# A chunked attention feeding a two-layer network: value products by chunk on 64 partitions, in a TensorE step of their own

## The chip, the cores and the metric

The kernel runs on one core of a Trainium2 chip. A core has TensorE (PE; its weight loads are shown apart, as PEld), VectorE (DVE), ScalarE (ACT), GpSimd (POOL) and SyncE (SP, which issues the DMA transfers here). The metric is the time of one execution in device microseconds. All times are in microseconds (us) unless marked ns.

## The reference, cut to what matters

```python
# attention: batch 4, heads 8, sequence 768, head width 64, 8 memory keys
chunk, left_ctx, right_ctx = (32, 16, 8)
for c in range(768 // chunk):
    k_full = concat(mem_k, k[c_start - 16 : c_end + 8])      # 8 + 56 = 64 keys, fewer at the ends
    v_full = concat(mem_v, v[c_start - 16 : c_end + 8])
    scores = scale * q_c @ k_full.T
    a = exp(scores - max(scores))
    a = a / (sum(a) + 1e-09)
    out[c_start:c_end] = a @ v_full
x = out as 3072 tokens x 512
# two-layer network
h = x @ w_in                                  # 512 -> 2048
g = maximum(h, 0) + alpha * minimum(h, 0)
return g @ w_out                              # 2048 -> 512
```

Each chunk of 32 queries sees 64 keys (8 of the memory, 16 on the left, its own 32, 8 on the right). All is float32.

## The kernel before, in words

**Blocks, slices, units.** The 3072 tokens are 8 blocks of 384. The hidden width of 2048 is 16 slices of 128, so the network is 128 pairs (block, slice). One pair is: `up`, 12 matmuls that move 384 columns (L614, into `h_ps`); `below` and `bend` (ACT L623, DVE L626), which form `g`; a split of `g` into a high part `gh` (L632) and a low part `gl` (L636); and `down`, 9 matmuls that move 512 columns (L644, into the banks `o_ps`). Below, "a slice" is also the time that TensorE takes for one such pair. The attention of a block is 4 units, one for each pair of heads, 32 units in all. A unit's outputs are also split in two (`xh` on ACT L408, `xl` on DVE L412), and `up` of the block reads both. The weights arrive packed and are decoded once, slice by slice, by `decode` (DVE and ACT, L556 to L583), while block 0 is computed.

**Units 0 to 7** (blocks 0 and 1) are done by `windows` at the start, by products of all of TensorE's 128 rows: scores L271, transposes L480, values L493. Their queries, keys and values come as `early` (L424).

**Units 8 to 31** go through four steps. `head_products` makes the scores of 12 chunks and two heads (L289, 24 matmuls on 64 partitions, into two PSUM banks `s0` and `s1`). `scores` takes the maxima (DVE L299 to L313) and the exponentials (ACT L320). `weights` divides (DVE L334, L337, then POOL L340) and copies a part into a padded tile `e2` (ACT L344). `turn` transposes the weights on DVE into a zeroed tile `pt` (L361, 14 pieces from the list `PIECES`). Each tile of 96 queries then has a window of 128 keys, in which a chunk's 64 weights stand beside zeros. `value_products` (L375) makes 8 matmuls of 128 rows, 64 output columns and 96 moving columns into one bank `a`. `zero` clears `e2` and `pt` once on POOL.

**What sets the order.** Nothing is ordered by hand inside a slice. `Plan` takes steps with an engine, an assumed cost, what they read and write, and a due time, and sends them in the order of a list schedule; each engine then runs its own list strictly in that order. `ORDER` lists the pairs (block, slice). Block 1's first `NJOINT` = 9 slices run interleaved with block 0's, `LAG` = 2 slices behind; their `down` adds up in the banks `s0`, `s1` and `a`, and ACT copies the sums out before block 2's units need these banks. `begins(u)` is the place at which a unit's scores are due; from block 3 on the four units of the next block begin at places -1, 3, 7 and 11. Weights and turn follow `DUE_WEIGHTS` = 3 slices after that and the values `DUE_VALUES` = 4 slices after, which is where the next unit begins. `attend` puts both into one TensorE step:

```python
def products():
    for u in olds:
        value_products(u)
    for u in news:
        head_products(u)
```

Of the kernel before, what the change touches and what calls it, by code (L numbers as in the profile page):

```python
# [9 lines left out]
F32 = mybir.dt.float32  # L10
# [55 lines left out]

NJOINT, LAG = 9, 2
ORDER = []
# [15 lines left out]

DUE_WEIGHTS, DUE_VALUES = 3, 4

# [70 lines left out]
def body(ctx: ExitStack, tc: tile.TileContext, qvw, kw, first, w_in, w_out, alpha, out):  # L157
# [26 lines left out]
    eye = const.tile([P, P], F32, name="eye")  # L184
    pts, zeroed = [], {}

# [33 lines left out]
    def sets(u):  # L220

        return u % NKB
# [21 lines left out]
    def load_v(u):  # L244
        blk, pr = divmod(u, NPAIR)

        def load():
            state[u]["v"] = ld.tile([P, NT, 2, D], F32, name="v_t")
            nc.sync.dma_start(out=state[u]["v"],
                              in_=qvw[blk, pr, :, BT:].rearrange("p (t h d) -> p t h d", t=NT, h=2))  # L250

        step(SP, 0.75, load, writes=["v"])

# [23 lines left out]

    def head_products(u):

        st = state[u]  # L280
        st["s"] = [ps_s.tile([P, 512], F32, name="s_ps", tag=f"s{h2}")[:, :NJ * KW].rearrange("p (n k) -> p n k", n=NJ)
                   for h2 in range(2)]
        for n in range(NJ):
            for g in range(4):
                t, j = SLOT[(g, n)]
                c = t * NJ + j
                for h2 in range(2):
                    rows = slice(h2 * D, (h2 + 1) * D)
                    nc.tensor.matmul(  # L289
                        out=st["s"][h2][g * CH:(g + 1) * CH, n],  # L290
                        lhsT=qs[sets(u)][rows, c * CH:(c + 1) * CH],
                        rhs=kbs[sets(u)][rows, t, STARTS[j]:STARTS[j] + KW],
                        start=True, stop=True,
                    )
# [35 lines left out]
    def weights(u):  # L330
        st = state[u]

        def guard():
            nc.vector.tensor_scalar(out=st["den"], in0=st["den"], scalar1=1e-9, scalar2=None, op0=ALU.add)  # L334

        def inverse():
            nc.vector.reciprocal(out=st["den"], in_=st["den"])  # L337

        def scale():
            nc.gpsimd.tensor_tensor(out=st["e"], in0=st["e"], in1=st["den"].broadcast_to([P, NJ * 2, KW]),  # L340
                                    op=ALU.mult)

        def spread():
            nc.scalar.copy(out=zeroed["e2"][:, :, NM:NM + CH], in_=st["e"][:, :, :CH])  # L344
# [4 lines left out]
        step(ACT, 0.37, spread, reads=e_keys(u), writes=["e2"], rest=due(u, DUE_WEIGHTS))  # L349

    TURNS = [(g, j, n0, n1, t0) + piece
             for g in range(4)
             for j, n0, n1, t0 in ([(g, 0, NJ, 0)] if g < NJ else [(n, n, n + 1, NT - 1) for n in range(NJ)])
             for piece in PIECES[j]]
    TURNS.sort(key=lambda x: x[5])

    def turn(u):
        st = state[u]

        def go(g, j, n0, n1, t0, src, half, quad):  # L360
            nc.vector.transpose(  # L361
                out=pts[u % NPT][quad * CH:(quad + 1) * CH, j, t0:t0 + n1 - n0].rearrange("p t h q -> p (t h) q"),
                in_=(st["e"], zeroed["e2"])[src][g * CH:(g + 1) * CH, 2 * n0:2 * n1, half * CH:(half + 1) * CH],
            )

        for i, x in enumerate(TURNS):
            step(DVE, 0.37 if x[3] - x[2] > 1 else 0.235, partial(go, *x), reads=["e2"] if x[5] else e_keys(u),
                 writes=[("pt", u % NPT, i)], rest=due(u, DUE_WEIGHTS))

    def value_products(u):  # L370
        st = state[u]
        st["a"] = ps_a.tile([P, 512], F32, name="a_ps", tag="a")
        for t in range(NT):
            for h2 in range(2):
                nc.tensor.matmul(  # L375
                    out=st["a"][h2 * D:(h2 + 1) * D, t * TQ:(t + 1) * TQ],
                    lhsT=st["v"][:, t, h2, :],
                    rhs=pts[u % NPT][:, :, t, h2, :],
                    start=True, stop=True,
                )  # L380

    def attend(place, olds, news):

        def products():
            for u in olds:
                value_products(u)
            for u in news:
                head_products(u)

        reads, writes = [], []  # L390
        for u in olds:
            reads += ["v"] + [("pt", u % NPT, i) for i in range(len(TURNS))]
            writes.append("a")
        for u in news:
            reads += [("q", sets(u)), ("k", sets(u))]
            writes += [("s", 0), ("s", 1)]
# [3 lines left out]
    def split(u, ak="a"):  # L400

        st = state[u]

        slot = u % NX

        def high():
            st["xh"] = xp.tile([P, BT], F32R, name="xh", tag=f"xh{slot}")
            nc.scalar.copy(out=st["xh"], in_=st["a"][:, :BT])  # L408

        def low():  # L410
            xl = xp.tile([P, BT], F32R, name="xl", tag=f"xl{slot}")
            nc.vector.tensor_tensor(out=xl, in0=st["a"][:, :BT], in1=st["xh"].bitcast(F32), op=ALU.subtract)  # L412
            xs[u] = (st["xh"], xl)

        xh, xl = ("xh", slot), ("xl", slot)
        step(ACT, 0.48, high, reads=[ak], writes=[xh])
        step(DVE, 0.56, low, reads=[ak, xh], writes=[xl])

# [11 lines left out]
    def windows(u):  # L430
# [56 lines left out]
        def values():  # L487
            pool, tag = (ps_o, "o2") if u % 2 else (ps_a, "a")
            st["a"] = pool.tile([P, 512], F32, name="a_ps", tag=tag)
            v = early[u % NSET][:, NQ + NT * NKT:].rearrange("p (t h d) -> p t h d", t=NT, h=2)  # L490
            for t in range(NT):
                for h2 in range(2):
                    nc.tensor.matmul(  # L493
                        out=st["a"][h2 * D:(h2 + 1) * D, t * TQ:(t + 1) * TQ],
                        lhsT=v[:, t, h2, :],
                        rhs=st["et"][:, t // 2, :, t % 2, h2, :],
                        start=True, stop=True,
                    )
# [12 lines left out]
        step(PE, 0.85, values, reads=[("q", u % NKB), ("fv", u % NSET)], writes=[ak], rest=due(u, 1))  # L511
        split(u, ak)
# [88 lines left out]
    def hidden(blk, f, first_f, last_f):  # L601
# [51 lines left out]
        def add_up():  # L653
            for ks in [[k] for k in range(NK)] if f < 2 else [list(range(NK))]:
                step(PE, 0.521 * len(ks), partial(up, ks),
                     reads=[("w", 0, f, 0), ("w", 0, f, 1)] + [(x, x_slot + k) for k in ks for x in ("xh", "xl")],
                     writes=[hk], rest=rest(place))
# [66 lines left out]
    for u in range(NWIN):  # L724
        unit_begins(u)
    step(POOL, 3.0, zero, writes=["e2"] + [("pt", i, j) for i in range(NPT) for j in range(len(TURNS))] + [("ew", i) for i in range(NPT)])
    for f in range(NF - NSET, NF):
# [48 lines left out]
def _layout(q, k, v, mem_k, mem_v, moe_w_in, moe_w_out, moe_alpha):  # L776
# [17 lines left out]
    for h in range(2):  # L794
# [3 lines left out]
    kfirst = kfirst.reshape(NBLK, NPAIR, P, NT * NKT)[:nwin]  # L798
    vparts = vwin.reshape(NBLK, NPAIR, P, NV)
    return dict(  # L800
        qvw=np.concatenate([qT.reshape(NBLK, NPAIR, P, BT), vparts], axis=3),
        kw=np.ascontiguousarray(kwin).reshape(NBLK, NPAIR, P, NT, NKT),
# [21 lines left out]
```

## Time and profile before

| | before |
|---|---|
| median of 3 runs | 614.57 (614.47 to 614.58) |
| the profiled execution's own time | 614.44 |
| its span in the profile | 612.7 |
| TensorE matmuls busy | 604.1 (99%) |
| TensorE weight loads busy | 532.5 (87%) |
| VectorE busy | 405.0 (66%) |
| ScalarE busy | 215.4 (35%) |
| GpSimd busy | 34.3 (6%) |

The span is the time between the first and the last instruction that the profiler saw. The profiled execution lies 0.13 under the median and 1.7 over its own span. A matmul in the profile has a start and a modelled end; consecutive ones overlap, so what a group costs TensorE is read from its first start to the next group's first start. A float32 matmul shows as two passes, each with its own weight load: 8 value matmuls are 16 records, 24 score matmuls are 48. In a row of the timeline the columns are start, length, engine, line, operation, output and inputs, array tile (rows*columns), shape of the moving operand, count, and in brackets an idle time and what ended it.

### The profile page before, as it was taken

To read this page: it belongs to the slowest core of one execution; us is meant where nothing else is said; L and a number is where in the kernel's file an instruction comes from. 1 tells how busy PE (TensorE), PEld (TensorE's weight loads), DVE (VectorE), ACT (ScalarE), POOL (GpSimd) and SP (SyncE) were. 2 spreads that over 40 slices of the span, in tenths; PEclk is the share of its full clock that TensorE was granted. 3 is DMA by queue.
4 is the path that set the end of the run, shared out by engine and by line. 5 is a ranking of instruction groups with operands and counts; after the bars stand their busy time and mean duration, and the time that the engine had idled before them with its cause. 6 is when DMAs were issued, how large, how long until landed. Compare 5 with 4: busy or idle time off the path is not lost.

```text
span 612.7 us, 11586 instructions
## 1 busy us (share of the span) xinstructions
PE 604.1 (99%) x4619; PEld 532.5 (87%) x4622; DVE 405.0 (66%) x1012; ACT 215.4 (35%) x596; POOL 34.3 (6%) x61
## 2 busy tenths in 40 slices
PE   8999999999999999999999999999999999999997
PEld 4779999888888888989888889888889888989996
DVE  5899899767877656766566766556766656633332
ACT  3798787544322222222223122332123222121111
POOL 3320000000000000000000000000000000000000
PEclk9999999999999999999999999999999999999999
DMA  8999300013121111201112001221012100010001
GB/s 351 355 404 407 152 0 1 24 41 123 46 101 49 50 49 50 77 25 50 49 50 101 26 25 49 83 67 50 19 31 101 50 18 18 1 53 1 0 1 51
DMA packets 20934, 48.99 MB, mean 80 GB/s; under 512 B 2448, under 2 KB 5520, under 8 KB 20880
## 3 DMA queue, kind: packets, MB, share of 16 engines
q1 hardware_dynamic: 20880, 48.25, 22.1%
q8 instruction: 36, 0.59, 0.4%
q14 instruction: 18, 0.15, 0.1%
HBM read 41.95 MB, written 6.29 MB: 79 GB/s over the span
## 4 chain that ended last, share of the span: by engine, by line
PE 95%; DMA 2%; DVE 1%; ACT 1%; SPq 0%; issue 0%; DVEq 0%; ACTq 0%
PE h_ps L614 44%; PE o_ps L644 44%; PE a_ps L375 3%; PE s_ps L289 3%; DMA early<-first 2%; PE s_ps L271 0%; PE a_ps L493 0%; PE o_ps L480 0%; DVE w_t L564 0%; ACT qk L485 0%; DVE a L572 0%; SPq L424 0%; ACT a L556 0%; ACT xh L408 0%; PE o_ps L257 0%; DVE w_t L568 0%
## 5 line engine op out<-in xcount | busy, mean ns | idle before, releaser
L614 PE MATMUL h_ps<-xh,w 128*128 128x384 f32 x1024 | 261.7, 336 | 0.0
L644 PE MATMUL o_ps<-w,gh 128*128 128x512 f32 x768 | 240.8, 395 | 0.0
L614 PEld LDWEIGHTS h_ps<-xh,w 128*128 128x128 f32 x1024 | 185.7, 188 | 4.1
L614 PE MATMUL h_ps<-xl,w 128*128 128x384 f32 x512 | 175.0, 342 | 1.2 <-DVE xl L412 1.2
L644 PEld LDWEIGHTS o_ps<-w,gh 128*128 128x128 f32 x768 | 144.1, 188 | 27.7
L623 ACT ACTIVATE g<-h_ps 128x384 f32<-128x384 f32 x128 | 63.4, 495 | 251.8 <-PE h_ps L614 245.6
L644 PE MATMUL o_ps<-w,gl 128*128 128x512 f32 x384 | 149.9, 390 | 0.0
L626 DVE SCALAR_TENSOR_TENSOR g<-g,rise,h_ps 128x384 f32<-128x384 f32 x128 | 78.4, 613 | 97.5 <-ACT g L623 96.7
L361 DVE STREAM_TRANSPOSE pt<-e 32x192 f32<-32x192 f32 (+1 forms) x336 | 99.6, 301 | 11.9 <-POOL e L340 6.6
L614 PEld LDWEIGHTS h_ps<-xl,w 128*128 128x128 f32 x512 | 96.2, 188 | 7.8 <-DVE xl L412 1.3
L644 PEld LDWEIGHTS o_ps<-w,gl 128*128 128x128 f32 x384 | 72.2, 188 | 12.2
L636 DVE TENSOR_TENSOR gl<-g,gh 128x384 fp32r<-128x384 f32 x128 | 71.2, 557 | 5.8 <-ACT gh L632 2.4
L632 DVE CAST gh<-g 128x384 fp32r<-128x384 f32 x104 | 37.3, 360 | 54.4 <-PE o_ps L644 52.7
L320 ACT ACTIVATE e<-s_ps,mx 128x64 f32<-128x64 f32 x144 | 43.3, 321 | 39.6 <-DVE mx L313 39.6
L340 POOL TENSOR_TENSOR e<-e,den 128x384 f32<-128x384 f32 x24 | 19.9, 830 | 467.1 <-DVE den L337 467.1
L408 ACT CAST xh<-a_ps 128x384 fp32r<-128x384 f32 x32 | 15.5, 483 | 53.1 <-PE a_ps L375 49.5
L320 ACT ACTIVATION_READ_ACCUMULATOR e<-s_ps,mx 128x1 f32 x144 | 30.7, 213 | 0.0
L375 PEld LDWEIGHTS a_ps<-pt,v_t 128*64 128x64 f32 x384 | 16.6, 136 | 8.5 <-issue 8.5
L375 PE MATMUL a_ps<-pt,v_t 128*64 128x96 f32 x384 | 21.1, 253 | 0.0
L583 DVE TENSOR_TENSOR w<-a,w 128x1024 fp32r<-128x1024 f32 (+1 forms) x18 | 19.7, 1098 | 1.2 <-ACT w L580 1.1
L572 DVE SCALAR_TENSOR_TENSOR a<-a,w_t 128x1024 int32<-128x1024 int32 (+1 forms) x18 | 20.1, 1116 | 0.2
L564 ACT COPY w_t<-w_t 128x512 int16<-128x512 int16 x14 | 19.4, 1387 | 0.1
(52 smaller groups left out, 277.1 us busy)
## 6 DMA issues: line engine op xcount, KB each, us to landing
w_t<-w_in SPq DMA_DIRECT2D x16, 512.0 KB, 10.2
w_t<-w_out SPq DMA_DIRECT2D x16, 512.0 KB, 10.2
qk<-kw SPq DMA_DIRECT2D x24, 272.0 KB, 3.7
v_t<-qvw SPq DMA_DIRECT2D x24, 256.0 KB, 2.7
out<-o_t SPq DMA_DIRECT2D x24, 256.0 KB, 2.1
early<-first SPq DMA_DIRECT2D x8, 656.0 KB, 6.9
qk<-qvw SPq DMA_DIRECT2D x24, 192.0 KB, 3.7
early<-first SPq DMA_DIRECT2D x8, 256.0 KB, 7.2
```

What stands on the lines that cost most here:

```text
L320: nc.scalar.activation(out=st["e"][:, i], in_=st["s"][h2][:, n], func=AF.Exp, scale=SCALE, bias=st["mx"][:, n, h2:h2 + 1], accum_out=st["d ...
L340: nc.gpsimd.tensor_tensor(out=st["e"], in0=st["e"], in1=st["den"].broadcast_to([P, NJ * 2, KW]), op=ALU.mult)
L361: nc.vector.transpose(out=pts[u % NPT][quad * CH:(quad + 1) * CH, j, t0:t0 + n1 - n0].rearrange("p t h q -> p (t h) q"), in_=(st["e"], zer ...
L375: nc.tensor.matmul(out=st["a"][h2 * D:(h2 + 1) * D, t * TQ:(t + 1) * TQ], lhsT=st["v"][:, t, h2, :], rhs=pts[u % NPT][:, :, t, h2, :], sta ...
L572: nc.vector.scalar_tensor_tensor(out=d["a"], in0=d["a"], scalar=3, in1=d["t"][:, :, :, 1], op0=ALU.logical_shift_left, op1=ALU.bitwise_or)
L583: nc.vector.tensor_tensor(out=d["w"][:, :, 1], in0=d["a"].bitcast(F32), in1=d["w"][:, :, 0].bitcast(F32), op=ALU.subtract)
L614: nc.tensor.matmul(out=h["ps"][:, :BT], lhsT=ws[f, 0][:, wk, k * P:(k + 1) * P], rhs=xs[first + k][xk], start=(k == 0 and n == 0), stop=(k ...
L623: nc.scalar.activation(out=h["g"], in_=h["ps"][:, :BT], func=AF.Relu, scale=-1.0)
L626: nc.vector.scalar_tensor_tensor(out=h["g"], in0=h["g"], scalar=rise[:, f:f + 1], in1=h["ps"][:, :BT], op0=ALU.mult, op1=ALU.add)
L632: copy(out=h["gh"], in_=h["g"])
L636: nc.vector.tensor_tensor(out=h["gl"], in0=h["g"], in1=h["gh"].bitcast(F32), op=ALU.subtract)
L644: nc.tensor.matmul(out=o_ps[tt], lhsT=h[gk][:, tt * P:(tt + 1) * P], rhs=ws[f, 1][:, wk], start=(f == first_f and i == 0), stop=(f == last ...
```

## The change

- **Values by chunk.** `value_products` multiplies each chunk's 64 weights with its own 64 values: 24 matmuls of 64 rows, 64 output columns and 32 moving columns. Chunks of the first half of the block use the array's upper 64 rows and bank `a`; chunks of the second half use the lower 64 rows and the upper columns of the bank that otherwise holds `s1`.
- **Less to prepare.** No padded tile: `e2`, its copy on ACT (`spread`) and the clearing on POOL (`zero`) go. `turn` has 8 transposes of 32x192 in place of 14 pieces. The values come from memory by chunk, so a unit's load `v_t` is 384 KB instead of 256 KB.
- **Split in two.** The outputs lie in two banks, so `xh` and `xl` of units 8 to 31 take two instructions of 192 columns each, on ACT and on DVE.
- **When.** `DUE_WEIGHTS` goes from 3 to 2 and `DUE_VALUES` from 4 to 3: the values are a step of their own, one slice ahead of the next unit's scores. Since both use the bank of `s1`, the scores wait for the split of its half.
- **Start.** `LAG` goes from 2 to 1: block 1's slice f follows block 0's slice f directly.
- **Assumed costs** of the planner for `attend` and `split` change with it.

```diff
-SLOT = {(g, n): ((n, g) if g < NJ else (NT - 1, n)) for g in range(4) for n in range(NJ)}
-PIECES = [[(0, 0, 0), (0, 1, 1)], [(0, 0, 1), (0, 1, 2)], [(1, 0, 2), (1, 1, 1), (0, 1, 3)]]
-NJOINT, LAG = 9, 2
+NJOINT, LAG = 9, 1
-DUE_WEIGHTS, DUE_VALUES = 3, 4
+DUE_WEIGHTS, DUE_VALUES = 2, 3
...
-            state[u]["v"] = ld.tile([P, NT, 2, D], F32, name="v_t")
+            state[u]["v"] = ld.tile([P, 2, NJ, 2, D], F32, name="v_t")
...
-    def head_products(u):
+    def head_products(u, second):
         st = state[u]
-        st["s"] = [ps_s.tile([P, 512], F32, name="s_ps", tag=f"s{h2}")[:, :NJ * KW].rearrange("p (n k) -> p n k", n=NJ)
-                   for h2 in range(2)]
+        st["s"] = [t[:, :NJ * KW].rearrange("p (n k) -> p n k", n=NJ)
+                   for t in (ps_s.tile([P, 512], F32, name="s_ps", tag="s0"), second)]
...
-        def spread():
-            nc.scalar.copy(out=zeroed["e2"][:, :, NM:NM + CH], in_=st["e"][:, :, :CH])
...
-        for i, x in enumerate(TURNS):
-            step(DVE, 0.37 if x[3] - x[2] > 1 else 0.235, partial(go, *x), reads=["e2"] if x[5] else e_keys(u),
+        def go(g, half):
+            quad = g // 2 * 2 + half
+            nc.vector.transpose(
+                out=st["pt"][quad * CH:(quad + 1) * CH, g % 2],
+                in_=st["e"][g * CH:(g + 1) * CH, :, half * CH:(half + 1) * CH],
+            )
+        for i in range(8):
+            step(DVE, 0.37, partial(go, i // 2, i % 2), reads=e_keys(u),
...
-        for t in range(NT):
-            for h2 in range(2):
-                nc.tensor.matmul(
-                    out=st["a"][h2 * D:(h2 + 1) * D, t * TQ:(t + 1) * TQ],
-                    lhsT=st["v"][:, t, h2, :],
-                    rhs=pts[u % NPT][:, :, t, h2, :],
-                    start=True, stop=True,
-                )
+        st["a"] = [(ps_a.tile([P, 512], F32, name="a_ps", tag="a")[:, :BT // 2], slice(0, BT // 2)),
+                   (second[:, BT // 2:BT], slice(BT // 2, BT))]
+        for b in range(2):
+            for n in range(NJ):
+                for h2 in range(2):
+                    for i in range(2):
+                        rows, c = slice(i * D, (i + 1) * D), b * NJ + n
+                        nc.tensor.matmul(
+                            out=st["a"][i][0][h2 * D:(h2 + 1) * D, c * CH:(c + 1) * CH],
+                            lhsT=st["v"][rows, b, n, h2, :],
+                            rhs=st["pt"][rows, b, n * 2 + h2],
+                            start=True, stop=True,
+                        )
...
-        step(PE, 0.85 * len(olds) + 0.67 * len(news) - (0.2 if olds and news else 0.0), products, reads=reads, writes=writes,
+        step(PE, 0.75 * len(olds) + 0.75 * len(news), products, reads=reads, writes=writes,
...
-        step(ACT, 0.48, high, reads=[ak], writes=[xh])
-        step(DVE, 0.56, low, reads=[ak, xh], writes=[xl])
+        for i, ak in enumerate(aks):
+            step(ACT, 0.48 if len(aks) == 1 else 0.34, partial(high, i), reads=[ak], writes=xh + xl if i == 0 else [xh[i]])
+        for i, ak in enumerate(aks):
+            step(DVE, 0.56 if len(aks) == 1 else 0.33, partial(low, i), reads=[ak, xh[i]], writes=[xl[i]])
...
-    def zero():
-        zeroed["e2"] = turned.tile([P, NJ * 2, KW], F32, name="e2", tag="e2")
-        nc.gpsimd.memset(zeroed["e2"], 0.0)
-        for i in range(NPT):
-            pts.append(turned.tile([P, NJ, NT, 2, CH], F32, name=f"pt{i}", tag=f"pt{i}"))
-            nc.gpsimd.memset(pts[i], 0.0)
...
-                 writes=[("s", 0), ("s", 1), "a"] if joint else [("o", tt) for tt in range(NTT)],
+                 writes=[("s", 0), ("s", 1), "a", "a1"] if joint else [("o", tt) for tt in range(NTT)],
```

The order of instructions that comes of it is shown at three places, before and after. In these rows a line of the changed kernel has another number: `up` is L601 there, `down` L631, the scores L280, the values L363, the splits L400 (`xh`) and L404 (`xl`), and the weight decode L551 to L570. A number behind a tile's name tells one use of the tile from the next.

**TensorE, at a unit's values and the next unit's scores.** Before:

```order
L644 MATMUL o_ps_2967<-w_1055,gl_3309 128x512
L644 MATMUL o_ps_2967<-w_1055,gh_3306 128x512 x2
L375 MATMUL a_ps_3362<-pt0_649,v_t_3228 64x96 x8
L289 MATMUL s_ps_3371<-qk1_155 32x64
L289 MATMUL s_ps_3372<-qk1_155 32x64
```

After (the last two of 24 value matmuls, one `up`, the first two of 24 score matmuls):

```order
L363 MATMUL a_ps_3277<-pt_3224,v_t_3115 64x32
L363 MATMUL s_ps_3276<-pt_3224,v_t_3115 64x32
L601 MATMUL h_ps_3306<-xl_2302,w_1059 128x384
L601 MATMUL h_ps_3306<-xh_2301,w_1059 128x384 x2
L601 MATMUL h_ps_3306<-xl_2476,w_1059 128x384
L601 MATMUL h_ps_3306<-xh_2475,w_1059 128x384 x2
L601 MATMUL h_ps_3306<-xl_2696,w_1059 128x384
L601 MATMUL h_ps_3306<-xh_2695,w_1059 128x384 x2
L601 MATMUL h_ps_3306<-xl_2902,w_1059 128x384
L601 MATMUL h_ps_3306<-xh_2901,w_1059 128x384 x2
L280 MATMUL s_ps_3328<-qk0_154 32x64
L280 MATMUL s_ps_3327<-qk0_154 32x64
```

Before, 22 of the 24 units have their values directly ahead of another unit's scores. After, none has; one `up` of 12 matmuls lies between them (in block 2's units, where they are packed closer, an `up`, a `down` or both).

**VectorE, at the end of the windows.** The tiles `xl` here are those of units 4 to 7, `w_t`, `a` and `w` those of the weight decode. Before:

```order
L412 TENSOR_TENSOR xl_619<-a_ps_550,xh_589 128x384
L412 TENSOR_TENSOR xl_627<-a_ps_591,xh_612 128x384
L564 COPY w_t_488<-w_t_488 128x512
L583 TENSOR_TENSOR w_638<-a_525,w_638 128x512
L568 TENSOR_SCALAR w_t_488<-w_t_488 128x1024
L572 SCALAR_TENSOR_TENSOR a_617<-a_617,w_t_488 128x1024
L626 SCALAR_TENSOR_TENSOR g_670<-g_670,rise_151,h_ps_606 128x384
L636 TENSOR_TENSOR gl_696<-g_560,gh_679 128x384
L412 TENSOR_TENSOR xl_700<-a_ps_654,xh_690 128x384
L412 TENSOR_TENSOR xl_703<-a_ps_681,xh_698 128x384
```

After:

```order
L404 TENSOR_TENSOR xl_622<-a_ps_589,xh_621 128x384
L570 TENSOR_TENSOR w_625<-a_558,w_625 128x512
L404 TENSOR_TENSOR xl_645<-a_ps_627,xh_644 128x384
L570 TENSOR_TENSOR w_658<-a_532,w_658 128x512
L404 TENSOR_TENSOR xl_666<-a_ps_647,xh_665 128x384
L623 TENSOR_TENSOR gl_681<-g_607,gh_673 128x384
L551 COPY w_t_507<-w_t_507 128x512
L613 SCALAR_TENSOR_TENSOR g_700<-g_700,rise_151,h_ps_602 128x384
L555 TENSOR_SCALAR w_t_507<-w_t_507 128x1024
L623 TENSOR_TENSOR gl_719<-g_700,gh_706 128x384
L559 SCALAR_TENSOR_TENSOR a_679<-a_679,w_t_507 128x1024
```

The decode of a further slice's weights (`w_t_488` before, `w_t_507` after) and one `g` and `gl` moved from ahead of the last `xl` to behind it.

**SyncE, the first transfers** (1312 elements a partition are a unit's queries and keys, 512 its values). Before:

```order
L424 DMA early_157<-first 128x1312 [waits DMAHW0_49,PE_49]
L533 DMA w_t_243<-w_in 128x1024
L424 DMA early_158<-first 128x1312 [waits DMAHW1_49,PE_49]
L424 DMA early_157<-first 128x512
L424 DMA early_159<-first 128x1312 [waits DMAHW2_49,PE_49]
L424 DMA early_158<-first 128x512
```

After:

```order
L418 DMA early_157<-first 128x1312 [waits DMAHW0_49,PE_49]
L418 DMA early_158<-first 128x1312 [waits DMAHW1_49,PE_49]
L418 DMA early_157<-first 128x512
L418 DMA early_159<-first 128x1312 [waits DMAHW2_49,PE_49]
L418 DMA early_158<-first 128x512
L520 DMA w_t_319<-w_in 128x1024
```

The first 512 KB of weights moved behind four more loads of the windows.

More of the change, by code (lines that the diff above doesn't have):

```diff
@@ L348, in weights @@
         step(POOL, 0.86, scale, reads=den_keys(u), writes=e_keys(u), rest=due(u, DUE_WEIGHTS))
[L349 to L355, printed above, removed]
     def turn(u):
         st = state[u]
-        def go(g, j, n0, n1, t0, src, half, quad):
+        def go(g, half):
+            if (g, half) == (0, 0):
+                st["pt"] = turned.tile([P, 2, NJ * 2, CH], F32, name="pt", tag=f"pt{u % NPT}")
+            quad = g // 2 * 2 + half
@@ L370, in value_products @@
-    def value_products(u):
+                out=st["pt"][quad * CH:(quad + 1) * CH, g % 2],
+                in_=st["e"][g * CH:(g + 1) * CH, :, half * CH:(half + 1) * CH],
+            )
+        for i in range(8):
+            step(DVE, 0.37, partial(go, i // 2, i % 2), reads=e_keys(u),
+                 writes=[("pt", u % NPT, j) for j in range(8)] + [("ew", u % NPT)] if i == 0 else [("pt", u % NPT, i)], rest=due(u, DUE_WEIGHTS))
+    def value_products(u, second):
         st = state[u]
-        st["a"] = ps_a.tile([P, 512], F32, name="a_ps", tag="a")
-        for t in range(NT):
-            for h2 in range(2):
-                nc.tensor.matmul(
-                    out=st["a"][h2 * D:(h2 + 1) * D, t * TQ:(t + 1) * TQ],
-                    lhsT=st["v"][:, t, h2, :],
-                    rhs=pts[u % NPT][:, :, t, h2, :],
-                    start=True, stop=True,
-                )
+        st["a"] = [(ps_a.tile([P, 512], F32, name="a_ps", tag="a")[:, :BT // 2], slice(0, BT // 2)),
[11 more added lines that the diff above has]
+                        )
@@ L382, in attend @@
     def attend(place, olds, news):
         def products():
+            second = ps_s.tile([P, 512], F32, name="s_ps", tag="s1")
             for u in olds:
-                value_products(u)
+                value_products(u, second)
             for u in news:
-                head_products(u)
-        reads, writes = [], []
+                head_products(u, second)
+        reads, writes = [], ["a1", ("s", 1)]
         for u in olds:
-            reads += ["v"] + [("pt", u % NPT, i) for i in range(len(TURNS))]
+            reads += ["v"] + [("pt", u % NPT, i) for i in range(8)]
@@ L488, in values @@
             pool, tag = (ps_o, "o2") if u % 2 else (ps_a, "a")
-            st["a"] = pool.tile([P, 512], F32, name="a_ps", tag=tag)
+            a = pool.tile([P, 512], F32, name="a_ps", tag=tag)
+            st["a"] = [(a[:, :BT], slice(0, BT))]
             v = early[u % NSET][:, NQ + NT * NKT:].rearrange("p (t h d) -> p t h d", t=NT, h=2)
```

46 lines of the change are left out of this document (22 added, 24 removed).

## The prediction

> **What bounds the kernel now.** I read the page's busy times and its chain of waits first, then the sums by stretch of time, then TensorE's timeline around one unit's step, the single lines' durations, and the timelines of all engines in the first 40 us.
>
> ```profile
> span 612.7 us, 11586 instructions
> PE 604.1 (99%) x4619; PEld 532.5 (87%) x4622; DVE 405.0 (66%) x1012; ACT 215.4 (35%) x596; POOL 34.3 (6%) x61
> PE 95%; DMA 2%; DVE 1%; ACT 1%; SPq 0%; issue 0%; DVEq 0%; ACTq 0%
> ...
> 14.10:38.80 24.70, 22.23 (x279) 17.57 (x278) 21.89 (x47) 19.65 (x39) 9.64 (x21) 1.00 0.97 372
> ...
> 38.80:612.70 573.90, 570.19 (x4194) 507.99 (x4194) 375.91 (x945) 190.63 (x549) 19.91 (x24) 1.00 0.18 61
> ```
>
> The two stretches show length, then PE, PEld, DVE, ACT and POOL busy, the granted clock, the DMA share and GB/s. From 38.8 on TensorE is idle for 573.90 - 570.19 = 3.7 us, which is the last store; the clock is 1.00. So whatever this change does there counts only as TensorE time: work taken from DVE, ACT or POOL is worth nothing, and TensorE time is worth all of itself. Before 38.8 it is different: TensorE idles for 24.70 - 22.23 = 2.5 us after 14.1, and DVE (21.89) is as full as TensorE.
>
> **The change part by part. The values' own time.** One step of values and scores, an `up` and a `down` from the chain of waits, and one step of scores alone:
>
> ```profile
> 274.78 0.63 PE L644 MATMUL o_ps<-w,gh 128*128 128x512 f32 x2
> 275.34 0.88 PE L375 MATMUL a_ps<-pt,v_t 128*64 128x96 f32 x16
> 276.15 0.73 PE L289 MATMUL s_ps<-qk 64*32 64x64 f32 x48
> 276.81 0.44 PE L614 MATMUL h_ps<-xl,w 128*128 128x384 f32 x1
> 277.09 0.51 PE L614 MATMUL h_ps<-xh,w 128*128 128x384 f32 x2
> ...
> 58.90 2.10 PE h_ps L614 x12
> 61.00 2.08 PE o_ps L644 x9
> ...
> 119.04 0.51 PE L614 MATMUL h_ps<-xh,w 128*128 128x384 f32 x2
> 119.48 0.72 PE L289 MATMUL s_ps<-qk 64*32 64x64 f32 x48
> 120.14 0.50 PE L644 MATMUL o_ps<-w,gl 128*128 128x512 f32 x1
> 120.47 0.62 PE L644 MATMUL o_ps<-w,gh 128*128 128x512 f32 x2
> ```
>
> Start to start, the values take 276.15 - 275.34 = 0.81 and the scores 276.81 - 276.15 = 0.66. A visit to small array tiles costs more than its body. In the last group the scores start 0.09 later than the next `up` matmul would (119.04 + 2 x 0.175 = 119.39; an `up` matmul follows the last after 2.10 / 12 = 0.175, a `down` matmul after 2.08 / 9 = 0.23), and the second matmul behind them comes 0.33 after the first instead of 0.23. That is 0.09 in and 0.10 out: 0.19 a visit. Values and scores together cost 0.81 + 0.66 + 0.19 = 1.66, the scores alone 0.85.
>
> After the change 22 units that shared a visit make two: 22 x 0.19 = 4.2 us more, if the bodies stay. Two units (of the 24) had their values alone already.
>
> The values' new body no row shows. Each of four array tiles gets 6 matmuls of two passes, so 12 rounds, each a weight load of 64 columns and 32 moving columns. Before there were 8 rounds on two tiles: 0.05 for the first load, 8 x 0.083, and 0.10 to leave. Nearest rows for a round:
>
> ```profile
> L271 PEld LDWEIGHTS s_ps<-early x192: 132/138/169, 5.0 to 22.6; 128*64 128x64 f32 x192
> ...
> L289 PEld LDWEIGHTS s_ps<-qk x1152: 102/106/108, 119.5 to 515.6; 64*32 64x32 f32 x192
> ...
> 21.94 0.34 PE L271 MATMUL s_ps<-early 128*64 128x64 f32 x4
> ...
> 21.94 0.51 PE L271 MATMUL s_ps<-early 128*64 128x64 f32 x10
> ```
>
> The windows' scores (L271, two tiles) load 64 columns and move 64. The group's end goes from 0.34 with 4 passes to 0.51 with 10, so three rounds take 0.17: 0.057 to 0.058 a round. That is a little over the 0.055 of moving 64 columns (0.083 x 64 / 96). It is also what the load lasts: a load of 64 columns takes 138 ns against 106 ns for 32, so 32 columns more are 32 ns, and 64 columns hold the tile for 55 to 64 ns. Halving the moving columns therefore shortens a round only until the load ends it. With 0.058: 0.05 + 11 x 0.058 + 0.03 + 0.02 (four tiles start one after another) + 0.10 = 0.84.
>
> The other end is the scores' row: the same 24 matmuls in 48 passes, loads half as wide, and still 0.66, of which rounds explain only 0.05 + 6 x 0.055 + 0.10 = 0.48. The rest looks like the rate at which matmuls are handed over; then the values can't go under 0.66 less the shorter last round, 0.63. I take 0.84, since L271 has the same load width and the load is what repeats. So: (0.84 + 0.19 + 0.85 - 1.66) x 22 + 0.03 x 2 = **+4.9 us**; at 0.63 it would be 0.01 x 22 - 0.18 x 2 = -0.1.
>
> The Trainium skill ("TensorEngine Tiling (Array Packing)", Overview, Theoretical Speedup) gives up to twice the speed for a contraction of 64 rows or less. On the old body that would be 0.41, and the sum of this part -5.5 us. No row here has such a gain: the scores, on eight tiles, need 0.66 for fewer multiplications than the values.
>
> **The start.** Rows of TensorE, then of DVE:
>
> ```profile
> 15.41 0.92 PE L271 MATMUL s_ps<-early 128*64 128x64 f32 x24 [0.67 <-DMA early<-first]
> ...
> 18.33 0.88 PE L493 MATMUL a_ps<-qk,early 128*64 128x96 f32 x16 [0.37 <-DMA early<-first]
> ...
> 38.81 0.44 PE L614 MATMUL h_ps<-xl,w 128*128 128x384 f32 x1 [1.15 <-DVE xl L412]
> ...
> 33.29 1.51 DVE L564 COPY w_t<-w_t 128x512 int16<-128x512 int16 x1 [0.19 <-ACT a L556]
> ...
> 35.18 0.85 DVE L568 TENSOR_SCALAR w_t<-w_t 128x1024 int32<-128x1024 int32 x1
> 36.07 1.23 DVE L572 SCALAR_TENSOR_TENSOR a<-a,w_t 128x1024 int32<-128x1024 int32 x1
> 37.21 0.61 DVE L626 SCALAR_TENSOR_TENSOR g<-g,rise,h_ps 128x384 f32<-128x384 f32 x1
> 37.73 0.55 DVE L636 TENSOR_TENSOR gl<-g,gh 128x384 fp32r<-128x384 f32 x1
> 38.20 1.02 DVE L412 TENSOR_TENSOR xl<-a_ps,xh 128x384 fp32r<-128x384 f32 x2
> ```
>
> The brackets are the three stalls that name a cause: 0.67 + 0.37 for the windows' loads, 1.15 for the last two `xl`. All three are touched. The loads of `early` go ahead of the first weights, and five DVE instructions (1.51 + 0.85 + 1.23 + 0.61 + 0.55, 4.7 us) move behind the last `xl`. With LAG 1 TensorE then has four slices on the weights of slices 0 and 1, instead of three, before it needs slice 2's. Best case: all 2.5 us of idle time go. Worst: the moved decode becomes the wait, with one more `g` and `gl` ahead of slice 2's weights, 0.61 + 0.55 = 1.2 us lost. DVE's whole work up to there is nearly the same and its order is only better for the windows, so I take most of the three named stalls, 2.0 of 2.2: **-2.0 us**. What is late next is slice 2's decode.
>
> **What I cost at nothing.**
>
> ```profile
> L361 DVE STREAM_TRANSPOSE pt<-e 32x192 f32<-32x192 f32 x168 | 61.8, 368 | 9.2 <-POOL e L340 6.6
> L361 DVE STREAM_TRANSPOSE pt<-e 32x64 f32<-32x64 f32 x168 | 37.7, 233 | 2.7
> L344 ACT COPY e<-e 128x192 f32<-128x192 f32 x24 | 8.3, 347 | 14.6 <-POOL e L340 14.6
> L310 DVE TENSOR_REDUCE mx<-s_ps 128x3 f32<-128x192 f32 x48 | 17.2, 359 | 1.6
> ...
> 275.85 0.56 DVE L636 TENSOR_TENSOR gl<-g,gh 128x384 fp32r<-128x384 f32 x1
> ...
> 276.27 0.48 ACT L408 CAST xh<-a_ps 128x384 fp32r<-128x384 f32 x1 [2.42 <-PE a_ps L375]
> ...
> 282.71 0.83 POOL L340 TENSOR_TENSOR e<-e,den 128x384 f32<-128x384 f32 x1 [17.56 <-DVE den L337]
> ...
> v_t<-qvw SPq DMA_DIRECT2D x24, 256.0 KB, 2.7
> early<-first SPq DMA_DIRECT2D x8, 656.0 KB, 6.9
> ```
>
> Transposes fall from 7 x 0.368 + 7 x 0.233 = 4.2 to 8 x 0.368 = 2.9 us a unit, ACT's 0.35 copy and POOL's clearing go: off the path, worth 0 while TensorE is full.
>
> *The new wait.* The scores wait for the split of the values' second half, with one `up` (2.10) between. After the values end, `xh` starts 0.12 later (276.27 against 276.15), two halves take 2 x 0.35 (a 192-column copy on ACT), the last `xl` half 0.36 (a 192-column pass on DVE over PSUM), with some 0.1 at each hand-over: about 1.4 us. DVE has finished `gl` by then (276.41). So 0.7 us is to spare; a stall would stand in front of the scores and everything behind them on TensorE, 22 times.
>
> *Weights a slice earlier.* From the scores' start to POOL's product is 282.71 + 0.83 - 276.15 = 7.4 us; 8 transposes (2.9) and two sets of `g`, `gh` and `gl` on DVE (about 1.5 each) make 13.3. The values come after 0.85, four `down` (2.08 each) and three `up`: 15.5. Covered by 2 us.
>
> *Loads.* `v_t` grows to 384 KB; 2.7 us for 256 KB, and 6.9 even for 656 KB in the crowded start, against four slices (over 16 us). On SyncE it waits for the values, and what queues behind it are loads for a later unit.
>
> **The sum.** 614.44 + 4.9 - 2.0 = 617.3 for the profiled execution, which lies 0.13 under the median: **617.5 us**.
>
> **The rivals.**
> *The values are handed over, not loaded, at their limit* (0.63): the part is -0.1 and the start's 2.0 is all: 614.57 - 2.1 = 612.5, faster. For it: something other than rounds sets the scores' 0.66. Against: L271's loads. It decides below a body of about 0.73, where this part, 4.2 - 24 x 0.08 = 2.3, is about what the start gives; there the time would not change (614.9).
> *A tile's round lasts only as long as its moving columns* (0.028): a body of 0.05 + 11 x 0.028 + 0.03 + 0.10 = 0.49, a part of -0.13 x 22 - 0.32 x 2 = -3.5, 609.1. Against: the scores. The page's doubling would be this, at 607.
> *The start gives nothing*: slice 2's decode takes over the stall. 614.57 + 4.9 = 619.5, or 620.7 with the 1.2.
> *A new wait before the scores*: each 0.3 us that the split overruns its 0.7 of slack costs 22 x 0.3 = 6.6, so 624.
>
> **How the numbers follow.** A difference of 0.2% is 1.2 us, about what can be told from no change. Forecast: 0.54, with its own range 616.0 to 619.8 (start between -2.5 and 0, body 0.80 to 0.86). Handed over at the limit: 0.20. In between: 0.09. Moving columns alone: 0.03. Start gives nothing: 0.09. New wait: 0.05. Faster: 0.03 and 0.18 of the 0.20; the same: the 0.09, 0.02 of the forecast, 0.02 of the 0.20; slower: the rest. That is 0.21, 0.13 and 0.66. The range leaves out the fastest rival and the ends of the slow ones: 612.3 to 619.8.
>
> **What would show it.** Values' start to the next group's start: 0.84 (0.63 or 0.49 for the rivals). 24 visits by values, each with 0.09 and 0.10 around it, none beside scores. No PE wait on DVE `xl` before scores. TensorE's last stall of the start some 2 us earlier in its work, the next one, if any, at slice 2's weights. I am wrong if a load of 64 columns on half the rows is quicker than on all of them, which no row here tests.

## The result, and the profile after

The changed kernel takes **620.15 us** (median of 4 runs, 619.78 to 620.57) against 614.52 for the kernel before in the same comparison: a ratio of 1.0094, 95% interval 1.0082 to 1.0105, or 5.6 us more. The forecast was slower, but 3.0 more, and the time lies 0.35 over the top of its range. The profiled execution took 620.08 with a span of 618.3, so the 5.6 us (618.3 - 612.7) are all in the span. One execution among those below, in experiment 3, took 1182.56 us; the ratios leave it out, and its profile is not read.

The page's span, busy times and chain, its rows of the values' loads and transfers, and the sums by stretch (length; PE, PEld, DVE, ACT, POOL busy; clock, DMA share, GB/s) of the kernel after:

```profile
span 618.3 us, 12982 instructions
PE 610.4 (99%) x5390; PEld 534.2 (86%) x5390; DVE 379.3 (61%) x892; ACT 210.4 (34%) x596; POOL 32.0 (5%) x58
PE 96%; DVE 2%; issue 0%; ACT 0%; ACTq 0%
L363 PEld LDWEIGHTS a_ps<-pt,v_t 64*64 64x64 f32 x576 | 18.8, 134 | 8.6 <-issue 8.3
v_t<-qvw SPq DMA_DIRECT2D x24, 384.0 KB, 3.1
...
14.10:38.80 24.70, 24.70 (x299) 19.67 (x296) 21.11 (x48) 19.22 (x39) 7.77 (x18) 1.00 0.96 350
38.80:618.30 579.50, 573.76 (x4957) 507.93 (x4955) 351.93 (x826) 187.32 (x551) 19.91 (x24) 1.00 0.20 67
```

DVE fell from 405.0 to 379.3 and ACT from 215.4 to 210.4, as the change intends, and the time rose all the same: TensorE is still what everything waits for. Its idle time moved. Between 14.1 and 38.8 it has none left (24.70 of 24.70; before, 2.5 us were idle). After 38.8 it has 579.50 - 573.76 = 5.7 us instead of 3.7, and the list of waits has one new row there, which accounts for the 2.0 more:

```profile
PE o_ps L631 <- DVE gl L623: 2.1, 3, 1.1
```

(us in total, times, longest.) Three times `down` waits for `gl`. No such row stood in the profile before.

TensorE's timeline at one unit's values, after (24 matmuls, 48 passes; the middle left out):

```profile
277.62 0.63 PE L631 MATMUL o_ps<-w,gh 128*128 128x512 f32 x2
278.18 0.24 PE L363 MATMUL a_ps<-pt,v_t 64*64 64x32 f32 x1
278.18 0.24 PE L363 MATMUL s_ps<-pt,v_t 64*64 64x32 f32 x1
278.19 0.24 PE L363 MATMUL a_ps<-pt,v_t 64*64 64x32 f32 x1
278.19 0.24 PE L363 MATMUL s_ps<-pt,v_t 64*64 64x32 f32 x1
278.25 0.22 PE L363 MATMUL a_ps<-pt,v_t 64*64 64x32 f32 x1
...
278.31 0.22 PE L363 MATMUL a_ps<-pt,v_t 64*64 64x32 f32 x1
...
278.37 0.22 PE L363 MATMUL a_ps<-pt,v_t 64*64 64x32 f32 x1
...
279.01 0.44 PE L601 MATMUL h_ps<-xl,w 128*128 128x384 f32 x1
279.29 0.51 PE L601 MATMUL h_ps<-xh,w 128*128 128x384 f32 x2
```

Four passes start together, one on each array tile, and the next four 0.06 later (278.25, .31, .37). The values take 279.01 - 278.18 = 0.83 (median of the 24 units 0.832; before 0.811). They begin 0.10 after the next `down` matmul would (277.62 + 2 x 0.23 = 278.08), and behind them the second `up` matmul comes 0.28 after the first instead of 0.175. A visit costs 0.19 or 0.2, as priced.

Where the 5.6 us are, by the two timelines:

| | us |
|---|---|
| 22 more visits to small array tiles, 22 x 0.19 | +4.2 |
| the values' body, 24 x (0.832 - 0.811) | +0.5 |
| `down` waits for `gl`, three times (idle 2.1; start to start some 2.4) | +2.4 |
| the start | -1.5 |
| sum | 5.6 |

The start's term is read so: from the first TensorE instruction behind the windows, 38.81 before and 35.21 after, the `up` matmuls already done are taken off, 30 before and 18 after, at 0.1745 each. That leaves 33.57 and 32.07. The windows' last values and what follows them, after, and the windows' last values before:

```profile
34.40 0.88 PE L488 MATMUL a_ps<-qk,early 128*64 128x96 f32 x16
35.21 0.44 PE L601 MATMUL h_ps<-xl,w 128*128 128x384 f32 x1
...
36.77 0.88 PE L493 MATMUL a_ps<-qk,early 128*64 128x96 f32 x16
```

The windows' last values start 2.4 us sooner (34.40 against 36.77), but TensorE did 12 `up` matmuls fewer among them (2.1 us), and the stall of 1.15 behind them is gone: 2.4 - 2.1 + 1.2 = 1.5.

**How the three waits come about.** All lie in block 2's units, which begin two slices apart (3, 5, 7 and 9 places behind block 1's ninth slice) and not four. TensorE at all three, then ACT and DVE around them, after:

```profile
128.78 0.50 PE L631 MATMUL o_ps<-w,gl 128*128 128x512 f32 x1 [0.69 <-DVE gl L623]
...
131.73 0.22 PE L363 MATMUL s_ps<-pt,v_t 64*64 64x32 f32 x1
...
134.22 0.52 PE L601 MATMUL h_ps<-xh,w 128*128 128x384 f32 x2
...
140.14 0.50 PE L631 MATMUL o_ps<-w,gl 128*128 128x512 f32 x1 [1.08 <-DVE gl L623]
...
153.04 0.47 PE L631 MATMUL o_ps<-w,gl 128*128 128x512 f32 x1 [0.31 <-DVE gl L623]
```

```profile
134.77 0.32 ACT L400 CAST xh<-a_ps 128x192 fp32r<-128x192 f32 x1 [3.11 <-PE h_ps L601]
```

```profile
126.24 1.91 DVE L345 STREAM_TRANSPOSE pt<-e 32x192 f32<-32x192 f32 x5
128.16 1.03 DVE L623 TENSOR_TENSOR gl<-g,gh 128x384 fp32r<-128x384 f32 x2
...
135.12 0.36 DVE L404 TENSOR_TENSOR xl<-a_ps,xh 128x192 fp32r<-128x192 f32 x1 [2.87 <-ACT xh L400]
135.40 0.35 DVE L404 TENSOR_TENSOR xl<-s_ps,xh 128x192 fp32r<-128x192 f32 x1
135.78 2.67 DVE L345 STREAM_TRANSPOSE pt<-e 32x192 f32<-32x192 f32 x7
138.49 0.61 DVE L613 SCALAR_TENSOR_TENSOR g<-g,rise,h_ps 128x384 f32<-128x384 f32 x1
139.13 0.36 DVE L619 CAST gh<-g 128x384 fp32r<-128x384 f32 x1
139.53 0.56 DVE L623 TENSOR_TENSOR gl<-g,gh 128x384 fp32r<-128x384 f32 x1
...
151.85 0.38 DVE L345 STREAM_TRANSPOSE pt<-e 32x192 f32<-32x192 f32 x1
...
152.34 0.55 DVE L623 TENSOR_TENSOR gl<-g,gh 128x384 fp32r<-128x384 f32 x1
```

DVE takes its list strictly in order. At 126.24 five transposes (1.91) stand ahead of the `gl` that the next `down` needs, and TensorE stands still for 0.69. The second wait has a longer chain. Unit 8's values are done at 131.9, but its `xh` goes into the tile of unit 0 (eight tiles are taken in turn), and block 0's last `up` still reads that one until 134.74. ACT waits 3.11 for it. DVE's `xl`, which stands ahead of everything else in its list, waits 2.87 for `xh`; then come seven transposes, a `g` and a `gh`, and only at 139.53 the `gl` that `down` has been waiting for. The `down` at 153.04 waits for a `gl` that starts at 152.34, again behind transposes. Before, the same `xh` of unit 8 comes 6 us later and waits for its own values only:

```profile
139.87 0.88 PE L375 MATMUL a_ps<-pt,v_t 128*64 128x96 f32 x16
...
140.80 0.48 ACT L408 CAST xh<-a_ps 128x384 fp32r<-128x384 f32 x1 [0.91 <-PE a_ps L375]
```

There unit 8's values are done at 140.7, here at 131.9: two slices sooner, not one. `LAG` 1 brings block 2 forward by one slice and `DUE_VALUES` the values by another. In the list `ORDER`, counted from 0, block 1's ninth slice has place 18 before and 17 after, and block 0's last slice 24 in both. So unit 8's values belong to place 18 + 3 + 4 = 25 before and to 17 + 3 + 3 = 23 after, ahead of block 0's last slice.

### The profile page after: what moved, and what is told of

It is laid out like the page before. It is cut to its first block, busy times and chain, and to the rows that moved or that the text cites. A ratio compares the mean times of both kernels' runs of the same rounds, so it can differ in the third digit from the quotient of the medians.

```text
span 618.3 us, 12982 instructions
## 1 busy us (share of the span) xinstructions
PE 610.4 (99%) x5390; PEld 534.2 (86%) x5390; DVE 379.3 (61%) x892; ACT 210.4 (34%) x596; POOL 32.0 (5%) x58
## 4 chain that ended last, share of the span: by engine, by line
PE 96%; DVE 2%; issue 0%; ACT 0%; ACTq 0%
PE h_ps L601 43%; PE o_ps L631 43%; PE a_ps L363 3%; PE s_ps L280 2%; PE s_ps L249 1%; PE s_ps L263 1%; PE a_ps L488 1%; DVE pt L345 1%; PE o_ps L474 1%; PE s_ps L363 1%; PE o_ps L249 0%; DVE gl L623 0%; DVE mx L301 0%; DVE g L613 0%; DVE e L441 0%
## 5 line engine op out<-in xcount | busy, mean ns | idle before, releaser
L601 PE MATMUL h_ps<-xh,w 128*128 128x384 f32 x1024 | 261.8, 337 | 0.0
L631 PE MATMUL o_ps<-w,gh 128*128 128x512 f32 x768 | 240.3, 394 | 0.0
L601 PEld LDWEIGHTS h_ps<-xh,w 128*128 128x128 f32 x1024 | 185.8, 188 | 3.9
L601 PE MATMUL h_ps<-xl,w 128*128 128x384 f32 x512 | 175.2, 342 | 0.0
L631 PEld LDWEIGHTS o_ps<-w,gh 128*128 128x128 f32 x768 | 144.2, 188 | 27.5
L631 PE MATMUL o_ps<-w,gl 128*128 128x512 f32 x384 | 152.7, 398 | 2.1 <-DVE gl L623 2.1
L601 PEld LDWEIGHTS h_ps<-xl,w 128*128 128x128 f32 x512 | 96.3, 188 | 5.3
L631 PEld LDWEIGHTS o_ps<-w,gl 128*128 128x128 f32 x384 | 72.2, 188 | 16.7 <-DVE gl L623 2.3
L345 DVE STREAM_TRANSPOSE pt<-e 32x192 f32<-32x192 f32 x192 | 70.8, 369 | 9.2 <-POOL e L331 5.7
L400 ACT CAST xh<-a_ps 128x192 fp32r<-128x192 f32 (+1 forms) x32 | 11.5, 359 | 56.8 <-PE s_ps L363 52.2
L363 PEld LDWEIGHTS a_ps<-pt,v_t 64*64 64x64 f32 x576 | 18.8, 134 | 8.6 <-issue 8.3
L363 PE MATMUL a_ps<-pt,v_t 64*64 64x32 f32 x576 | 21.5, 221 | 0.0
L363 PE MATMUL s_ps<-pt,v_t 64*64 64x32 f32 x576 | 21.5, 221 | 0.0
L570 DVE TENSOR_TENSOR w<-a,w 128x1024 fp32r<-128x1024 f32 (+1 forms) x18 | 20.0, 1114 | 0.3 <-ACT w L567 0.3
```

Source lines behind the costliest of these rows:

```text
L345: nc.vector.transpose(out=st["pt"][quad * CH:(quad + 1) * CH, g % 2], in_=st["e"][g * CH:(g + 1) * CH, :, half * CH:(half + 1) * CH],)
L363: nc.tensor.matmul(out=st["a"][i][0][h2 * D:(h2 + 1) * D, c * CH:(c + 1) * CH], lhsT=st["v"][rows, b, n, h2, :], rhs=st["pt"][rows, b, n * ...
L570: nc.vector.tensor_tensor(out=d["w"][:, :, 1], in0=d["a"].bitcast(F32), in1=d["w"][:, :, 0].bitcast(F32), op=ALU.subtract)
L601: nc.tensor.matmul(out=h["ps"][:, :BT], lhsT=ws[f, 0][:, wk, k * P:(k + 1) * P], rhs=xs[first + k][xk], start=(k == 0 and n == 0), stop=(k ...
L631: nc.tensor.matmul(out=o_ps[tt], lhsT=h[gk][:, tt * P:(tt + 1) * P], rhs=ws[f, 1][:, wk], start=(f == first_f and i == 0), stop=(f == last ...
```

## The experiments

In each comparison the kernel before had 614.44.

**1. The changed kernel with the old due times** (values back in one step with the next unit's scores; the new matmuls, transposes, split and `LAG` 1 stay).

```diff
-DUE_WEIGHTS, DUE_VALUES = 2, 3
+DUE_WEIGHTS, DUE_VALUES = 3, 4
```

> The changed kernel with DUE_WEIGHTS, DUE_VALUES = 3, 4 again: the 24 value matmuls stand directly ahead of the next unit's scores, 27 visits to small tiles instead of 48. Theory (visits cost 0.19 each, the value body is 0.83 instead of 0.81, three waits of `down` for `gl` in block 2's units cost 2.1, the start gives 1.2): 21 x 0.19 = 4.0 less than the changed kernel, and 2.1 less if the waits come from the weights and values being a slice early: 620.15 - 4.0 - 2.1 = 614.0. Rival (the waits come from block 2 beginning a slice sooner, with LAG 1): they stay, 616.1. Rival (a visit costs nothing, the values' form is what costs): 620.

Measured: 613.82 (613.17 to 614.67, 11 runs), ratio 0.9991 (0.9982 to 1.0000), span 611.7. There are 27 visits instead of 48, the body stays at 0.832, and `down` waits for no `gl` (unit 8's values belong to place 24). So everything that the change loses hangs on the two due times: 620.15 - 613.82 = 6.3, which is 21 visits (4.0) and the waits. What is left of the change then gains nothing that can be told from no change.

**2. The kernel before with the new due times alone.**

```diff
-DUE_WEIGHTS, DUE_VALUES = 3, 4
+DUE_WEIGHTS, DUE_VALUES = 2, 3
```

> The kernel before with DUE_WEIGHTS, DUE_VALUES = 2, 3 alone: its 8 value matmuls in a step of their own, 47 visits instead of 26, the old start (LAG 2). Theory: 21 x 0.19 = 4.0 more than before and no more, 618.5. Rival (the step is free and the small-tile form costs): 614.5. Rival (a slice early also makes `down` wait for `gl` in block 2's units): 620.6.

Measured: 619.48 (619.31 to 619.67), ratio 1.0082 (1.0068 to 1.0096). That is 5.0 more, with 47 visits: 21 x 0.19 = 4.0, and one wait more than I had expected, of another kind:

```profile
PE a_ps L375 <- DVE xl L412: 1.1, 1, 1.1
```

In block 2 the old values have only the one bank `a`, and a unit's values come while the unit ahead is still being split out of it. The price of a visit thus holds with the old matmuls too: it belongs to the step of its own, not to the chunks.

**3. `LAG` 1 alone, in the kernel before** (run twice).

```diff
-NJOINT, LAG = 9, 2
+NJOINT, LAG = 9, 1
```

> The kernel before with LAG = 1 alone: values and scores still joined, 26 visits. Theory: the start gives 1.2, 613.3, with no stall in block 2's units. Rival (LAG 1 itself brings the waits there, since block 2's units begin a slice sooner while block 0's last `up` still holds the outputs of units 0 to 3): 613.3 + 2.1 = 615.4. Rival (the start's gain came from the padded tile that was dropped, not from LAG): 614.5 or more.

> The kernel before with LAG = 1 alone, for its profile. Theory: 613.4, TensorE's windows done some 1.5 us sooner in its work than before, no wait of `down` for `gl` in block 2's units (their weights and values keep 3 and 4 slices). Rival (LAG 1 alone makes such waits): a stall of some 1 us there, and a gain at the start that is as much larger.

Measured: 613.44 both times, ratios 0.9980 (0.9971 to 0.9989) and 0.9983 (0.9974 to 0.9992). The profile read is the second run's (span 612.0); it shows no stall on `xl` behind the windows and no wait of `down` for `gl` later. So the new start alone is worth 1.0 us, and alone it makes none of the waits.

**4. The changed kernel with `LAG` 2.**

```diff
-NJOINT, LAG = 9, 1
+NJOINT, LAG = 9, 2
```

> The changed kernel with LAG = 2 again, all else as changed: 48 visits, old start. Theory: before + 4.7 (22 visits x 0.19, 24 x 0.02 of body) = 619.2, the start's 1.2 lost and the three waits of `down` gone, if it takes LAG 1 to bring them. Rival (the waits come from the weights and values being a slice early): 621.3, with the stalls at block 2's units.

Measured: 618.79 (618.74 to 618.96), ratio 1.0070 (1.0058 to 1.0083), with 48 visits and no wait of `down` for `gl`. This is the values' part of the change by itself: 4.35 us against 4.2 + 0.5 by its terms and 4.9 as forecast. The old stalls of the start are back:

```profile
15.66 0.92 PE L263 MATMUL s_ps<-early 128*64 128x64 f32 x24 [0.86 <-DMA early<-first]
18.43 0.88 PE L488 MATMUL a_ps<-qk,early 128*64 128x96 f32 x16 [0.20 <-DMA early<-first]
38.66 0.44 PE L601 MATMUL h_ps<-xl,w 128*128 128x384 f32 x1 [0.91 <-DVE xl L404]
```

With `LAG` 2 the first 512 KB of weights are back ahead of the windows' later loads, as in the kernel before, and the windows wait for loads again. The three late waits took `LAG` 1 together with the new due times: experiments 1 and 3 have the one, this one and experiment 2 the other, and none of them has the waits. In all four, unit 8's values belong to place 24.

**5. The changed kernel, block 2's units begun one slice later.**

```diff
-BEGIN = {2: (3, 5, 7, 9)}
+BEGIN = {2: (4, 6, 8, 10)}
```

> The changed kernel with LAG = 1 kept, and block 2's units begun one slice later (places 4, 6, 8, 10 instead of 3, 5, 7, 9), which is where they stood with LAG 2. 48 visits. Theory (the three waits of `down` for `gl` come from LAG 1 moving these units ahead of block 0's last `up`): they go, the start's gain stays, 620.15 - 2.1 = 618.0. Rival (they come from the weights and values being a slice early): they stay, 620.2.

Measured: 617.50 (617.34 to 618.09), ratio 1.0052 (1.0040 to 1.0065), with 48 visits still. The waits are gone, and unit 8's `xh` waits for its own values again, at about the time that it had in the kernel before:

```profile
139.33 0.32 ACT L400 CAST xh<-a_ps 128x192 fp32r<-128x192 f32 x1 [0.94 <-PE s_ps L363]
```

Unit 8's values belong to place 24 here too. So the three waits cost 620.15 - 617.50 = 2.65 us, about what the trace gives for them (2.4). Without them the change costs 3.06, about what had been forecast for all of it.

**6. Wider moving operands**: 20 of the 24 value matmuls move 64 columns instead of 32 (the second half is overwritten by the matmul whose place it is, or lands beside the outputs and is not read).

```diff
+bank = ps_a.tile([P, 512], F32, name="a_ps", tag="a")
+wide = [bank, second[:, BT // 2:]]
...
+m = 2 if n * 2 + h2 < 2 * NJ - 1 else 1
-    out=st["a"][i][0][h2 * D:(h2 + 1) * D, c * CH:(c + 1) * CH],
+    out=wide[i][h2 * D:(h2 + 1) * D, c * CH:c * CH + m * CH],
...
-    rhs=st["pt"][rows, b, n * 2 + h2],
+    rhs=st["pt"][rows, b, n * 2 + h2:n * 2 + h2 + m].rearrange("p x q -> p (x q)"),
```

> The changed kernel, in which 20 of a unit's 24 value matmuls move 64 columns instead of 32 (the next columns of the weights beside them, written where the next chunk overwrites them), with the same weight loads of 64 columns. Theory (a round lasts as long as the load of 64 columns, 0.058): the body grows only by the last round, from 0.83 to 0.83 to 0.87, the time by at most 24 x 0.04 = 1.0, 620.2 to 621.2. Rival (a round lasts as long as its moving columns, and 32 columns take longer than their share): the body grows by up to 10 x 0.028 = 0.28, the time by 6.7, 626.8. Rival (the matmuls are handed over no faster): nothing changes, and the starts lie as far apart as in the scores.

One unit's values and the `up` behind them, then weight loads of the same group (one row of every four):

```profile
279.36 0.27 PE L365 MATMUL a_ps<-pt,v_t 64*64 64x64 f32 x1
...
280.20 0.44 PE L603 MATMUL h_ps<-xl,w 128*128 128x384 f32 x1
...
279.41 0.13 PEld L365 LDWEIGHTS a_ps<-pt,v_t 64*64 64x64 f32 x1
...
279.47 0.14 PEld L365 LDWEIGHTS a_ps<-pt,v_t 64*64 64x64 f32 x1
...
279.53 0.14 PEld L365 LDWEIGHTS a_ps<-pt,v_t 64*64 64x64 f32 x1
```

Measured: 620.64 (620.52 to 621.49), ratio 1.0101 (1.0085 to 1.0116). The body is 0.84 (median 0.845): twice the moving columns cost 0.013. So the moving columns are not what a round lasts. The loads of a round start 0.06 after those of the round before it, as the matmuls did with 32 moving columns.

**7. Half the weight load**: the value matmuls load 32 of their 64 columns, so half of each output is left at zero; DVE clears the two banks first. One execution was timed.

```diff
+for a, _ in st["a"]:
+    nc.vector.memset(a, 0.0)
...
-    out=st["a"][i][0][h2 * D:(h2 + 1) * D, c * CH:(c + 1) * CH],
-    lhsT=st["v"][rows, b, n, h2, :],
+    out=st["a"][i][0][h2 * D:h2 * D + D // 2, c * CH:(c + 1) * CH],
+    lhsT=st["v"][rows, b, n, h2, :D // 2],
```

> The changed kernel, in which each value matmul loads only 32 of its 64 columns of values, so that half of each output is left at zero (DVE clears both banks ahead of the step, which may stall TensorE there; the time of the body alone counts). Same 24 matmuls, same 32 moving columns. Theory (a round lasts as long as the load): the body falls from 0.83 to the scores' rate of handing over, about 0.63; at half of each load 0.05 + 11 x 0.03 + 0.15 = 0.53 would be the floor. Rival (moving columns or the handing over set it): 0.83 stays.

Values, the `up` behind them, and the loads by shape:

```profile
277.68 0.21 PE L365 MATMUL a_ps<-pt,v_t 64*32 64x32 f32 x1
...
277.74 0.19 PE L365 MATMUL a_ps<-pt,v_t 64*32 64x32 f32 x1
...
277.77 0.19 PE L365 MATMUL a_ps<-pt,v_t 64*32 64x32 f32 x1
...
277.80 0.19 PE L365 MATMUL a_ps<-pt,v_t 64*32 64x32 f32 x1
...
278.11 0.19 PE L365 MATMUL s_ps<-pt,v_t 64*32 64x32 f32 x1
278.24 0.45 PE L603 MATMUL h_ps<-xl,w 128*128 128x384 f32 x1
...
L365 PEld LDWEIGHTS s_ps<-pt,v_t 64*32 64x32 f32 x576 | 12.2, 107 | 0.1
```

Measured: 615.73, span 613.9; the body falls from 0.832 to 0.553 (here 278.24 - 277.68 = 0.56), further than the 0.63 that I had expected, and 24 x 0.28 = 6.7 us go. Of these 4.4 show in the time. Once TensorE waits 0.7 for a clear, which also stretches that unit's values to 0.83, and the start of this execution, reckoned as in the table, ended 1.0 later (33.1 against 32.1): together some 2.0. The 48 passes now start within 0.43 us, and the rounds of four follow each other after 0.03 (277.74, .77, .80) where they took 0.06. So the width of the load sets the rounds at 64 columns. The output is as wide as the load, and the array tile in the records changes with it (64*32), so load width and output width were not told apart.

**8. The kernel before with `LAG` 1 and block 2 begun later**, both edits of 3 and 5.

> The kernel before with LAG = 1 and block 2's units begun one slice later (4, 6, 8, 10), so that they stand to block 0's last slices as before. Theory (LAG 1 gives about 1.5 at the start and block 2's units give nothing away): 613.0 to 613.4. Rival (the start's gain is used up by run-to-run differences in when the first loads land): 614.4.

Measured: 613.34 (612.42 to 614.12, 11 runs), ratio 0.9982 (0.9973 to 0.9991). It is the fastest kernel here, by 1.1 us on the kernel before, though not told apart from `LAG` 1 alone (613.44): where no wait stands, a later begin gains nothing.

## Why the prediction was right and wrong

**Right: TensorE time is what counts.** DVE and ACT lost 26 and 5 us of work, and neither shows in the time.

**Right: the visits.** 22 x 0.19 = 4.2 was the largest term. Experiment 2 shows it without the new matmuls (47 visits) and experiment 4 without the new start; experiment 1 takes it out again.

**Right: the values' body**, 0.84 forecast and 0.832 measured, and with the reason given, that the round is the weight load, borne out as far as the runs go. A load lasts 134 ns on half the rows; in the profile before the same 64 columns on all of them took 136:

```profile
L375 PEld LDWEIGHTS a_ps<-pt,v_t 128*64 128x64 f32 x384 | 16.6, 136 | 8.5 <-issue 8.5
```

So the condition under which I would have been wrong, a quicker load on half the rows, did not hold. Experiments 6 (more moving columns, nearly the same body) and 7 (half the load, two thirds of the body) point the same way, but for the output width, which changes with the load. The rivals fall: "moving columns alone" had 0.49 and falls by the measured 0.832 and by 6, and "handed over, not loaded", to which I had given 0.20, by 7, since the body there goes under the 0.63 that it named as a floor. The Trainium skill ("TensorEngine Tiling (Array Packing)", Overview, Theoretical Speedup) has up to twice the speed for a contraction of 64 rows or less; the body here went from 0.811 to 0.832, and only a narrower load brought it down.

**Right: no new wait of the scores for the split**, and the loads of 384 KB (3.1 us) hold nothing up.

**Wrong: "Weights a slice earlier", "covered by 2 us"**, costed at nothing. This is the step that failed, by 2.4 to 2.65 us, and with it the time left the range. The cover was worked out on the steady stretch, with a unit every four slices, and on the chain that ends at the values (weights, transposes and two sets of `g`, `gh` and `gl`). Block 2's units come every two slices, the first of them beside the last slices of block 0, where `LAG` 1 and the new due time together move the values by two slices. There a DVE list that runs in order puts a unit's transposes and splits ahead of a `gl`, and the tile that a split writes is still being read. The rival "a new wait before the scores" looked for a wait at 22 units, at the scores that follow the values into their bank; the real one came three times and hit `down`, whose `gl` only stood behind the moved work in DVE's list. Without it the forecast would have been right to the tenth: experiment 5, the change without the waits, is 617.50. But that is partly luck, since two terms were too large in opposite directions: +4.9 for the values, where experiment 4 has 4.35, and -2.0 for the start. The top of the range, 619.8, comes out of its terms only from 614.44, while the lower end takes 614.57; from there the top would be 619.95, and the time lies above that as well.

**Mis-sized: the start, -2.0.** It was -1.5 in the profiled execution, and in timed runs 1.0 (experiment 3) and 618.79 - 617.50 = 1.3 (experiments 4 and 5, in both of which unit 8 begins at place 21). The three named stalls did go. But TensorE ran fewer `up` matmuls among the windows, and of the 1.0 that the windows' loads had cost only some 0.3 came back (2.4 - 2.1 in the working above). Reckoned as in the table, the start ends between 31.6 and 33.2 in the seven profiles with `LAG` 1 and between 33.3 and 33.6 in the three with 2. What in the start varies so was not settled; some of those profiles show stalls of 0.2 to 0.5 on the windows' loads. The windows' first scores also differ, 1.55 after against 0.95 before; but experiment 2, with the old order of loads, has 1.55 too and a start of 33.3, so that alone does not set it. Whether the order of the loads or the order of the pairs brings the gain was not tried either.

## What to carry to other kernels

When a step is moved earlier, work out its cover not only on the steady stretch but at the place where the units stand closest, and ask of each in-order engine what stands *behind* the moved instructions and who waits for that; the tile that they write may still be in use there, too. Splitting small-tile TensorE work into steps of its own has a fixed price for each visit (0.19 us here), so keep such steps side by side. Narrower moving operands did not shorten a matmul group here whose rounds followed the width of the weight load.

## What the runs showed of the hardware that was not expected

Matmuls of four array tiles are handed over far faster than the scores' row had suggested: in experiment 7, 48 passes start within 0.43 us, and the body is 0.553, while the scores, with as many passes and loads as narrow, keep 0.654. What sets the scores' 0.654 is open; they move 64 columns, the values of experiment 7 move 32.

Doubling the moving columns from 32 to 64 on 20 of 24 matmuls was nearly free (0.832 to 0.845): with loads of 64 columns the rounds came 0.06 apart either way, and with loads of 32 columns 0.03. Whether each array tile is held by its own load for that long, or the four tiles share something that the loads take in turn, was not told apart.
